# Half as many transfers around a chunked RWKV-7 recurrence: loads by batch, other head pairs, one output transfer

## The chip, the cores and the metric

The kernel runs on one core of a Trainium2 chip. The metric is the device time of one execution in microseconds. The core has TensorE (PE), VectorE (DVE), ScalarE (ACT), GpSimd (POOL) and SyncE (SP), which here only issues transfers; each executes its instructions in order. Sixteen DMA engines move the data.

## The reference

Two parts. An RWKV-7 recurrence over 4 batches, 8 heads, 768 steps, heads of 40, then a feed-forward block with `h * cos(h)`:

```python
for t in range(S):                       # state: (B, H, D, D)
    y[:, :, t] = einsum('bhd,bhde->bhe', r_t, state)
    Sa = einsum('bhde,bhe->bhd', state, a_t)
    state = state * w_t[:, :, None, :] - einsum('bhd,bhe->bhde', Sa, b_t)
    state = state + einsum('bhd,bhe->bhde', v_t, k_t)
x = y.transpose(0, 2, 1, 3).reshape(B * S, H * D)    # 3072 x 320
h = x @ w_in                                         # 320 x 2048
out = (h * cos(h)) @ w_out                           # 2048 x 320
```

The six recurrence inputs are float32; the weights arrive in 64 bits and are converted on the chip.

## The kernel before, in words

The 768 steps are cut into 24 chunks of 32. A chunk holds the 32 steps of all 4 batches on the 128 partitions, and the heads, padded from 40 to 64 columns, in pairs: two heads fill the 128 rows of a transposed tile. In the tiles before, `nat_*` is `[P, 4, 2, 64]`, and the pair `j` consists of heads `j` and `j + 4` for `w`, `a`, `b`, `k` (loaded half by half, line 127), but of neighbours for `v` and `r` (line 122).

- `p1(c)` prepares two chunks without the state: `p1_w` transposes `w` (`wT`) and scans its products (`wp`, `wx`, `wc`); `p1_a` turns them back, takes the reciprocal `rw`, forms `aT` and `bn`; `p1_b` transposes `bn`; `p1_n` multiplies to `nps`, masks it to `nt`, and sends it through a DRAM tile `nd` into `u`, where each partition holds one 32x32 matrix of one head, batch and chunk.
- `inverse(c, part)` inverts the 128 triangular matrices of four chunks at once on VectorE (lines 319 and 323, 31 steps); `inv_end` sends the result through DRAM (`rd`) into `rt`.
- `p2_v`, `p2_k`, `p2_g` bring `k`, `v`, `r` of one chunk: `kn = k * rw` on POOL (line 338), the transposes `vT`, `rT`, `kT`, and the Gram matrices `ag` and the outer parts of `vvm`, in whose middle 40 columns the chunk's `v` stands (a second load of `v`, `load_vv`, line 133).
- `ch_t`, `ch_q`, `ch_x`, `ch_s`, `ch_z` are the chunk proper: they read the state in `qz`, apply `rt` (`sps`, `sm`), write the state back (`dps`; `qz` on VectorE and POOL, lines 480 and 481) and the output `yt` (lines 487 and 492). `yt` goes through a DRAM tile `xd` into `xT`, two chunks to a group (lines 498, 505, 507).
- The feed-forward block is cut into 192 pieces, `first_a`, `first_b` (matmuls `ph`) and two `second` (matmuls `po`) for each of 12 groups and 4 quarters of its columns. The last quarter of a group evicts `po` into `ot` and sends it out (line 556).
- `load_weights` loads 28 blocks of the weights on ACT's queue and converts them on VectorE, ACT and POOL (lines 173 to 191).

The order of TensorE is the program's (`manual_schedule`). Chunk `c` runs its five segments with, between them, `p2_*` of chunk `c + 1`, in the first two of every four chunks `p1` of two chunks of the next four, and then as many feed-forward pieces as are due; a piece of group `g` waits until chunk `2g + 2` is reached. In the third and fourth of every four chunks the next inverse is emitted. The order of the other engines and of SyncE's queue comes from a planner that goes by the instructions' modelled readiness and their place in the program. All transfers but the weights' are issued by SyncE.

Of the kernel before, what the change touches and what calls it, by code (L numbers as in the profile page):

```python
# [9 lines left out]
F32 = mybir.dt.float32  # L10
# [10 lines left out]
def kernel(  # L21
# [77 lines left out]
    def pick(t, offset, *dims):  # L99
# [3 lines left out]
    src = {"r": r, "k": k, "v": v, "w": w, "a": a, "b": b}  # L103

    padding = lambda t: t[:, :, :, D:]
    nat = {
        n: kept(f"nat_{n}", [P, 4, 2, DP], 2, 1.0 if n == "w" else 0.0, padding) for n in "wabkvr"
    }
# [46 lines left out]
    bn_b = kept("bn", [P, 4, 2, DP], 7, 0.0, padding)  # L155
    kn_b = kept("kn", [P, 4, 2, DP], 2, 0.0, padding)
# [75 lines left out]
    unpad = lambda t: t[:, :, :, :D]  # L232
# [44 lines left out]
    def p1_n(c):  # L277
# [20 lines left out]
        nd = dram.tile([P, 2, H, C], F32, tag="nd", name="nd")  # L298
        nc.sync.dma_start(nd.rearrange("p c h t -> p (c h t)"), nt.rearrange("p c e n -> p (c e n)"))
        for i in range(2):  # L300
            for g in range(4):
                p0 = 32 * ((c + i) % 4) + 8 * g
                nc.sync.dma_start(
                    G["u"][p0 : p0 + 8].rearrange("h (s t) -> h s t", s=C),
                    nd[blk[g], i].rearrange("s h t -> h s t"),
                )
# [18 lines left out]
    def inv_end(c):  # L325
        rd = dram.tile([P, C, C], F32, tag="rd", name="rd")
        nc.sync.dma_start(rd.rearrange("p s t -> p (s t)"), G["inv"])
        for i in range(4):
            rt = ring.tile([P, H, C], F32, tag="rt", name="rt")
            for g in range(4):  # L330
                p0 = 32 * i + 8 * g
                nc.sync.dma_start(rt[blk[g]], rd[p0 : p0 + 8].rearrange("h s t -> s h t"))
            G["rt", c + i] = rt


    def p2_v(c):
# [16 lines left out]
    def p2_g(c):  # L353
# [9 lines left out]
        for j in range(4):  # L363
# [13 lines left out]
            pick(vvm[c % 2], C + D, (C, 2), (2 * NV, HH), (1, C)), v1,  # L377
            su.unsqueeze(1).to_broadcast([P, 2, HH, C]), ALU.mult,
        )
        nc.scalar.copy(pick(vvm[c % 2], 0, (2 * NV - C, 2), (2 * NV, HH), (1, C)), v1)  # L380
# [13 lines left out]
    def ch_q(c):  # L394
        ps = at("qps")
        for i in range(2 * B):
            for pa in range(2):
                for e in range(2):
                    mm(
                        ps[full[pa], e, i * C : (i + 1) * C], G["s"][half[e], i, full[pa]],  # L400
                        G["rT", c][half[e], 2 * pa + i % 2, blk[i // 2]], i == 0,
                    )
        nc.scalar.copy(
            pick(qz, 0, (NZ - C, 2), (NZ, 2 * B), (1, C)),
            ps[:, :, : 2 * B * C].rearrange("p e (i t) -> p e i t", t=C),
        )

    def ch_x(c):
        ps = at("x0ps")
        for j in range(4):  # L410
            m, e = j // 2, j % 2
            for bb in range(B):
                for pa in range(2):
                    mm(
                        ps[blk[bb ^ pa], pa, j * N72 : (j + 1) * N72], G["ag", c][blk[bb], 4 * pa + j, :],
                        vvm[c % 2][blk[bb], 4 * pa + j, e * C : e * C + N72], j == 0,
                    )
        if c:
            for j in range(4):
                m, e = j // 2, j % 2  # L420
                for bb in range(B):
                    for pa in range(2):
                        mm(
                            ps[blk[bb ^ pa], pa, j * N72 : (j + 1) * N72],
                            G["aT", c][half[pa], j, blk[bb]],
                            qz[half[pa], bb, m, e * (NZ - N72) : e * (NZ - N72) + N72], False,
# [6 lines left out]
    def ch_s(c):  # L433
        ps = at("sps")
        x0 = G["x0"]
        for j in range(4):
            for bb in range(B):
                for pa in range(2):
                    g = bb ^ pa
                    mm(  # L440
                        ps[blk[bb], pa, j * N72 : (j + 1) * N72], G["rt", c][blk[g], 4 * pa + j, :],
                        x0[blk[g], pa, j * N72 : (j + 1) * N72], j == 0,
# [3 lines left out]
        for pa in range(2):  # L446
            nc.scalar.copy(
                pick(sm[:, pa], 0, (2 * N72, 2), (N72 + C, 2), (1, D)),
                ps[:, pa, : 4 * N72].rearrange("p (m n) -> p m n", m=2)[:, :, C : C + 2 * D].rearrange(
                    "p m (e d) -> p m e d", e=2  # L450
                ),
            )
            nc.vector.tensor_tensor(
                pick(sm[:, pa], D, (2 * N72, 2), (1, 2 * C)),
                pick(ps[:, pa], 0, (2 * N72, 2), (2 * N72 - C, 2), (1, C)),
                su.rearrange("p (m e) t -> p m e t", e=2), ALU.mult,
# [3 lines left out]
    def ch_z(c):  # L460
        ps = [at("dps") for _ in range(2)]
        sm = G["sm"]
        for s, n in ((0, kn_b[c % 2]), (1, bn_b[c % 7])):
            for j in range(4):
                for bb in range(B):
                    for pa in range(2):
                        o = C - C * (j % 2)
                        mm(
                            ps[bb // 2][full[pa], bb % 2, j * N72 : (j + 1) * N72], n[blk[bb], j, pa, :],
                            sm[blk[bb], pa, j, :] if s else vvm[c % 2][blk[bb], 4 * pa + j, o : o + N72],  # L470
# [3 lines left out]
        yt = sb2.tile([P, 4, B, C], F32, tag="yt", name="yt")  # L474
        for i in range(2):
            for bb in range(2 * i, 2 * i + 2):
                dp = ps[i][:, bb % 2]
                if c < NCH - 1:
                    z = pick(qz[:, bb], C, (NZ, 2), (DP, 2), (1, D))
                    nc.vector.tensor_tensor(z, pick(dp, 0, (2 * N72, 2), (N72 + C, 2), (1, D)), z, ALU.add)  # L480
                    nc.gpsimd.tensor_tensor(  # L481
                        z, z,
                        wc.rearrange("p (m e b) -> p m e b", m=2, e=2)[:, :, :, bb]
                        .unsqueeze(3).to_broadcast([P, 2, 2, D]),
                        ALU.mult,
                    )
                nc.vector.tensor_tensor(  # L487
                    yt.rearrange("p (m e) b t -> p m e b t", e=2)[:, :, :, bb],
                    pick(dp, D, (2 * N72, 2), (C, 2), (1, C)),
                    pick(qz[:, bb], 0, (NZ, 2), (NZ - C, 2), (1, C)), ALU.add,  # L490
                )
        nc.gpsimd.tensor_tensor(
# [48 lines left out]
    def second(g, j, i):  # L541
# [44 lines left out]
    with tc.manual_schedule(engines={mybir.EngineType.PE}):  # L586
        for seg in p1(0):
            seg()
        load(0, "kvr")
        load_vv(0)  # L590
        load_vv(1)
        load(2, "wab")
        load(3, "wab")
        for seg in p1(2):
            seg()
        load(4, "wab")
# [8 lines left out]
        START, done, n_seg = 4, 0, 0  # L605
        for c in range(NCH):
# [10 lines left out]
            for i, seg in enumerate(main):  # L617
# [3 lines left out]
                due = (c + (i + 1) / n - START) / (NCH - START) * len(pieces) * 0.97  # L621
# [3 lines left out]
            if c + 2 < NCH:  # L625
                load_vv(c + 2)
# [39 lines left out]
```

## Time and profile before

| | |
|---|---|
| median of 3 runs | 1186.43 us (1184.93 to 1189.02) |
| the profiled execution | 1181.81 us, its span 1180.1 us |
| mean granted TensorE clock | 0.808 |
| busy: PE, DVE, ACT, POOL | 838.5, 507.9, 344.0, 200.8 us (71, 43, 29, 17%) |
| transfers | 270372 packets, 65.68 MB, mean 56 GB/s; 244352 packets under 512 B |
| queue of SyncE and its DMA share | 266112 packets, 52.78 MB, 25.2% of 16 engines |

The span runs from the first to the last instruction; the rest of the execution's time lies around it. Busy shares are means over stages that differ: a start without feed-forward work (to about 180 us), four chunks without it (to about 300 us), the mixed part, and a last group after the last chunk. Matmuls are pipelined, so a busy TensorE is not at its peak.

### The profile page before, as it was taken

To read this page: it belongs to the slowest core of one execution; us is meant where nothing else is said; L and a number is where in the kernel's file an instruction comes from. 1 tells how busy PE (TensorE), PEld (TensorE's weight loads), DVE (VectorE), ACT (ScalarE), POOL (GpSimd) and SP (SyncE) were. 2 spreads that over 40 slices of the span, in tenths; PEclk is the share of its full clock that TensorE was granted. 3 is DMA by queue.
4 is the path that set the end of the run, shared out by engine and by line. 5 is a ranking of instruction groups with operands and counts; after the bars stand their busy time and mean duration, and the time that the engine had idled before them with its cause. 6 is when DMAs were issued, how large, how long until landed. Compare 5 with 4: busy or idle time off the path is not lost.

```text
span 1180.1 us, 37667 instructions
## 1 busy us (share of the span) xinstructions
PE 838.5 (71%) x16472; PEld 644.0 (55%) x16472; DVE 507.9 (43%) x1109; ACT 344.0 (29%) x651; POOL 200.8 (17%) x342
## 2 busy tenths in 40 slices
PE   2140025474688888888987896976977977979878
PEld 1030014363466666665765675755766765757656
DVE  5056985327153375334283335174334292222212
ACT  1011111121233433342432423332422332434323
POOL 1036453121020111111011011011012011020100
PEclk9975555755689988989888998888987986979879
DMA  3434452342412412333213333313332223110000
GB/s 73 61 74 112 118 132 59 49 73 44 85 36 38 80 26 40 82 63 52 51 39 46 76 55 48 58 35 53 74 58 40 52 37 67 35 33 18 16 24 12
DMA packets 270372, 65.68 MB, mean 56 GB/s; under 512 B 244352, under 2 KB 264320, under 8 KB 270208
## 3 DMA queue, kind: packets, MB, share of 16 engines
q1 hardware_dynamic: 266112, 52.78, 25.2%
q10 hardware_dynamic: 4096, 10.49, 2.9%
q8 instruction: 130, 2.13, 0.8%
q14 instruction: 34, 0.28, 0.1%
HBM read 49.02 MB, written 14.16 MB: 54 GB/s over the span
## 4 chain that ended last, share of the span: by engine, by line
PE 41%; SPq 22%; DVE 14%; DMA 7%; issue 7%; ACT 6%; POOL 3%; POOLq 0%; DVEq 0%; ACTq 0%
SPq L127 16%; PE ph L97 15%; PE po L97 13%; DVE inv_tmp L319 2%; DVE inv L323 2%; DVE rw L261 2%; PE x0ps L97 2%; PE dps L97 2%; ACT turns L536 1%; SPq L122 1%; PE bT L226 1%; PE nps L97 1%; PE gram L97 1%; ACT turns L535 1%; DVE wp L245 1%
## 5 line engine op out<-in xcount | busy, mean ns | idle before, releaser
L97 PE MATMUL po<-w_out_sb,gT 128*128 128x320 f32 x768 | 249.3, 479 | 0.0
L97 PE MATMUL ph<-xT,w_in_sb 128*128 128x256 f32 x768 | 202.9, 419 | 18.2 <-DMA xT<-xd 18.1
L97 PEld LDWEIGHTS po<-w_out_sb,gT 128*128 128x128 f32 x768 | 156.2, 211 | 71.6 <-issue 26.4
L97 PEld LDWEIGHTS ph<-xT,w_in_sb 128*128 128x128 f32 x768 | 159.9, 213 | 48.0 <-issue 11.0
L534 DVE SCALAR_TENSOR_TENSOR turns<-turns,ph 128x512 f32<-128x512 f32 x96 | 61.6, 682 | 276.5 <-ACT turns L533 276.5
L533 ACT ACTIVATE turns<-ph,rnd 128x512 f32<-128x512 f32 x96 | 60.7, 684 | 203.1 <-PE ph L97 203.1
L537 DVE TENSOR_TENSOR gT<-ph,turns 128x512 f32<-128x512 f32 x96 | 65.9, 690 | 63.8 <-ACT turns L536 63.5
L481 POOL TENSOR_TENSOR qz<-qz,wc 128x160 f32<-128x160 f32 x92 | 40.5, 461 | 257.4 <-DVE qz L480 257.0
L226 PE MATMUL vT<-ident,nat_v 128*128 128x128 f32 x96 | 18.8, 329 | 78.7 <-DMA nat_v<-in_v_dram 78.7
L319 DVE TENSOR_TENSOR inv_tmp<-u,inv 128x31 f32<-128x31 f32 (+15 forms) x186 | 70.8, 381 | 5.3
L323 DVE TENSOR_TENSOR inv<-inv,inv_tmp 128x31 f32<-128x31 f32 (+15 forms) x186 | 68.1, 366 | 5.0
L536 ACT ACTIVATE turns<-turns,half_pi 128x512 f32<-128x512 f32 x96 | 68.9, 722 | 2.3
L226 PE MATMUL wT<-ident,nat_w 128*128 128x128 f32 x96 | 17.5, 328 | 66.4 <-DMA nat_a<-in_a_dram 57.0
L535 ACT ACTIVATE turns<-turns 128x512 f32<-128x512 f32 x96 | 59.4, 624 | 10.3 <-DVE turns L534 10.3
L249 POOL COPY wx<-wp 128x496 f32<-128x496 f32 x24 | 14.4, 599 | 270.3 <-DVE wp L245 270.3
L338 POOL TENSOR_TENSOR kn<-nat_k,rw 128x320 f32<-128x320 f32 x24 | 21.1, 881 | 225.0 <-PE dps L97 199.0
L245 DVE TENSOR_TENSOR_SCAN wp<-w,w 128x512 f32<-128x512 f32 x24 | 29.8, 1242 | 67.9 <-ACT w L243 66.3
L226 PEld LDWEIGHTS vT<-ident,nat_v 128*128 128x128 f32 x96 | 12.8, 166 | 80.4 <-issue 79.7
L97 PE MATMUL gram<-aT,kT 40*32 40x32 f32 x1536 | 20.5, 226 | 49.1 <-DVE yt L487 33.3
L97 PE MATMUL ph<-xT,w_in_tail 64*128 64x256 f32 x384 | 54.8, 404 | 0.0
L261 DVE RECIPROCAL rw<-wn 128x320 f32<-128x320 f32 x24 | 51.6, 2149 | 4.5 <-PE wn L226 4.2
L226 PEld LDWEIGHTS wT<-ident,nat_w 128*128 128x128 f32 x96 | 12.6, 166 | 69.1 <-issue 63.8
(91 smaller groups left out, 1143.0 us busy)
## 6 DMA issues: line engine op xcount, KB each, us to landing
words<-in_moe_w_out_dram ACTq DMA_DIRECT2D x16, 320.0 KB
words<-in_moe_w_in_dram ACTq DMA_DIRECT2D x8, 512.0 KB
nat_w<-in_w_dram SPq DMA_DIRECT2D x192, 20.0 KB
nat_a<-in_a_dram SPq DMA_DIRECT2D x192, 20.0 KB
nat_b<-in_b_dram SPq DMA_DIRECT2D x192, 20.0 KB
nat_k<-in_k_dram SPq DMA_DIRECT2D x192, 20.0 KB
nat_v<-in_v_dram SPq DMA_DIRECT2D x96, 40.0 KB
nat_r<-in_r_dram SPq DMA_DIRECT2D x96, 40.0 KB
```

Of the source, the lines that this page charges most:

```text
L97: nc.tensor.matmul(o, lhsT=lhsT, rhs=rhs, start=start, stop=stop, skip_group_check=True)
L127: nc.sync.dma_start(t[:, :, e, :D], s[HH * e : HH * (e + 1)].rearrange("j t d -> t j d"))
L226: nc.tensor.transpose(ps[:, i * P : (i + 1) * P], x[:, i].rearrange("p e d -> p (e d)"), ident)
L245: nc.vector.tensor_tensor_scan(flat(wp), flat(w0), flat(w1), 0.0, ALU.mult, ALU.add)
L261: nc.vector.reciprocal(rw, unpad(ps[:, 0].rearrange("p (j a d) -> p j a d", a=2, j=4)))
L319: nc.vector.tensor_tensor(tmp, u[:, :j, j : j + 1].to_broadcast([P, j, C - j]), x[:, j : j + 1, j:].to_broadcast([P, j, C - j]), ALU.mult,)
L323: nc.vector.tensor_tensor(x[:, :j, j:], x[:, :j, j:], tmp, ALU.subtract)
L533: nc.scalar.activation(n, u, ACTF.Identity, bias=rnd, scale=1.0)
L534: nc.vector.scalar_tensor_tensor(n, n, -ROUND, u, ALU.add, ALU.subtract)
L535: nc.scalar.activation(n, n, ACTF.Abs)
L536: nc.scalar.activation(n, n, ACTF.Sin, bias=half_pi, scale=-2.0 * math.pi)
L537: nc.vector.tensor_tensor(G["gT", j][:, 2 * e : 2 * e + 2].rearrange("p f t -> p (f t)"), u, n, ALU.mult)
```

## The change

- Loads: all six inputs of a chunk are loaded with one transfer for each batch (`nat_*` is `[P, 8, ...]`). For `w`, `a`, `b`, `k` the pairs become neighbouring heads, `2j` and `2j + 1`. `v` and `r` are loaded unpadded, and POOL copies them into the padded tiles `vp` and `rp` in another pair order, so that the halves `f` of a pair are heads `i` and `i + 4`. The middle of `vvm` is a POOL copy of `nat_v`; `load_vv` is gone.
- The first loads come in another order: `w` of chunks 0 and 1, `a` of both on ACT's queue, `b`; then `w` of 2 and 3, `a` and `b` of both; `k`, `v`, `r` of chunk 0 only after `p1(2)` is emitted.
- Re-layout: `u`'s partitions are ordered by batch, chunk, head, so one transfer for each batch serves two chunks; `rt` becomes one tile for four chunks with one transfer for each batch.
- Output: one transfer for each output tile. `yt` has one buffer in place of two.
- The due rate of the feed-forward pieces: `SHARE` in place of 0.97.
- The indices of the chunk's matmuls follow the new pairs; their number and shapes stay.

The core of the diff:

```diff
-        n: kept(f"nat_{n}", [P, 4, 2, DP], 2, 1.0 if n == "w" else 0.0, padding) for n in "wabkvr"
+    nat = {n: kept(f"nat_{n}", [P, H, DP], 2, 1.0 if n == "w" else 0.0, padding) for n in "wabk"}
+    nat |= {n: kept(f"nat_{n}", [P, H, D], 2) for n in "vr"}
+    vp, rp = (kept(n, [P, H, DP], 1, 0.0, padding)[0] for n in ("vp", "rp"))
...
-    def load(c, names):
+    def load(c, names, via=nc.sync):
         for n in names:
             for i in range(B):
-                s = src[n][i, :, c * C : (c + 1) * C, :]
-                t = nat[n][c % 2][blk[i]]
-                if n in "vr":
-                    nc.sync.dma_start(
-                        t.rearrange("t i e d -> t (i e) d")[:, :, :D], s.rearrange("h t d -> t h d")
-                    )
-                else:
-                    for e in range(2):
-                        nc.sync.dma_start(
-                            t[:, :, e, :D], s[HH * e : HH * (e + 1)].rearrange("j t d -> t j d")
-                        )
-    def load_vv(c):
...
-    load(0, "wab")
-    load(1, "wab")
+                via.dma_start(
+                    nat[n][c % 2][blk[i], :, :D],
+                    src[n][i, :, c * C : (c + 1) * C, :].rearrange("h t d -> t h d"),
+                )
+    load(0, "w")
+    load(1, "w")
+    load(0, "a", nc.scalar)
+    load(1, "a", nc.scalar)
+    load(0, "b")
+    load(1, "b")
...
-        nd = dram.tile([P, 2, H, C], F32, tag="nd", name="nd")
-        for i in range(2):
-            for g in range(4):
-                p0 = 32 * ((c + i) % 4) + 8 * g
-                nc.sync.dma_start(
-                    G["u"][p0 : p0 + 8].rearrange("h (s t) -> h s t", s=C),
-                    nd[blk[g], i].rearrange("s h t -> h s t"),
-                )
+        nd = dram.tile([P, 2 * H, C], F32, tag="nd", name="nd")
+        for g in range(4):
+            p0 = 32 * g + 8 * (c % 4)
+            nc.sync.dma_start(
+                G["u"][p0 : p0 + 2 * H].rearrange("h (s t) -> h s t", s=C),
+                nd[blk[g]].rearrange("s h t -> h s t"),
+            )
...
-            rt = ring.tile([P, H, C], F32, tag="rt", name="rt")
-            for g in range(4):
-                p0 = 32 * i + 8 * g
-                nc.sync.dma_start(rt[blk[g]], rd[p0 : p0 + 8].rearrange("h s t -> s h t"))
+        rt = sb2.tile([P, 4, H, C], F32, tag="rt", name="rt")
+        for g in range(4):
+            nc.sync.dma_start(
+                rt[blk[g]].rearrange("s c h t -> s (c h) t"), rd[blk[g]].rearrange("h s t -> s h t")
+            )
...
+        for dst, m in ((vp, "v"), (rp, "r")):
+            nc.gpsimd.tensor_copy(
+                dst.rearrange("p (i f) d -> p f i d", f=2)[:, :, :, :D],
+                nat[m][c % 2].rearrange("p (f i) d -> p f i d", f=2),
+            )
+        nc.gpsimd.tensor_copy(vvm[c % 2][:, :, C : C + D], nat["v"][c % 2])
...
-        yt = sb2.tile([P, 4, B, C], F32, tag="yt", name="yt")
+        yt = sb1.tile([P, 4, B, C], F32, tag="yt", name="yt")
...
-                xd[4 * D * e : 4 * D * (e + 1)].rearrange("(j d) t -> d j t", j=4),
+                xd.rearrange("(j e d) t -> e d j t", e=2, d=D)[e],
...
-            for bb in range(B):
-                t0 = bb * S + (2 * g + i) * C
-                nc.sync.dma_start(out[t0 : t0 + C, :], ot[blk[bb], :])
+            t0 = (2 * g + i) * C
+            nc.sync.dma_start(out.rearrange("(b s) n -> b s n", b=B)[:, t0 : t0 + C, :], ot)
...
-        load(0, "kvr")
-        load_vv(0)
-        load_vv(1)
-        load(2, "wab")
-        load(3, "wab")
+        load(2, "w")
+        load(3, "w")
+        load(2, "ab")
+        load(3, "ab")
         for seg in p1(2):
             seg()
+        load(0, "kvr")
...
+        SHARE = len(pieces) * (1 - 1.4 / (NCH // 2)) / (NCH - START)
...
-                due = (c + (i + 1) / n - START) / (NCH - START) * len(pieces) * 0.97
+                due = (c + (i + 1) / n - START) * SHARE
```

## Rows read from the trace of the kernel before

**Rows 1.** The page, part 4: the chain that ended last, shares of the span.
```profile
PE 41%; SPq 22%; DVE 14%; DMA 7%; issue 7%; ACT 6%; POOL 3%; POOLq 0%; DVEq 0%; ACTq 0%
```
**Rows 2.** Waits of TensorE, whole span: waiter <- releaser: us in total, times, longest.
```profile
PE vT L226 <- DMA nat_v<-in_v_dram: 78.7, 4, 61.9
PE wT L226 <- DMA nat_a<-in_a_dram: 57.0, 6, 17.1
PE gram L97 <- DVE yt L487: 33.3, 13, 6.5
PE ph L97 <- DMA xT<-xd: 18.1, 5, 6.9
PE sps L97 <- DMA rt<-rd: 16.5, 3, 15.6
```
**Rows 3.** Windows: stretch, length, busy PE PEld DVE ACT POOL, clock, DMA, GB/s.
```profile
33.40:75.40 42.00, 9.37 (x164) 7.22 (x161) 8.52 (x8) 2.49 (x6) 3.20 (x6) 0.97 0.37 56
...
75.00:180.00 105.00, 13.32 (x444) 10.59 (x438) 81.59 (x173) 18.75 (x35) 59.16 (x84) 0.50 0.47 120
...
266.70:299.90 33.20, 13.13 (x469) 10.50 (x468) 20.22 (x61) 3.99 (x9) 3.98 (x7) 0.50 0.30 46
...
300.00:420.00 120.00, 100.86 (x1906) 77.52 (x1905) 41.61 (x70) 43.37 (x80) 15.47 (x28) 0.88 0.31 57
...
1104.50:1132.50 28.00, 16.21 (x717) 13.38 (x716) 5.07 (x19) 4.09 (x10) 4.27 (x6) 0.60 0.10 28
```
**Rows 4.** Timeline of SyncE's queue: start, us spent on the issues, transfer, count.
```profile
0.81 5.45 SPq L127 DMA_DIRECT2D nat_w<-in_w_dram  x8
...
40.85 4.15 SPq L133 DMA_DIRECT2D vvm<-in_v_dram  x8
...
64.09 3.70 SPq L127 DMA_DIRECT2D nat_b<-in_b_dram  x8
...
78.65 16.84 SPq L303 DMA_DIRECT2D u<-nd  x8
...
164.78 15.48 SPq L332 DMA_DIRECT2D rt<-rd  x16
```
**Rows 5.** Timeline of all engines: start, us, instruction, [idle before, releaser].
```profile
61.85 1.08 PE L226 MATMUL wT<-ident,nat_w 128*128 128x128 f32 x4 [10.25 <-DMA nat_a<-in_a_dram]
...
75.49 0.76 DVE L290 TENSOR_TENSOR nt<-nps,su 128x256 f32<-128x256 f32 x2 [3.17 <-PE nps L97]
...
116.75 0.85 DVE L319 TENSOR_TENSOR inv_tmp<-u,inv 128x31 f32<-128x31 f32 x1
...
166.74 0.41 PE L97 MATMUL sps<-x,rt 32*32 32x72 f32 x2 [15.55 <-DMA rt<-rd]
...
221.72 1.08 PE L226 MATMUL wT<-ident,nat_w 128*128 128x128 f32 x4 [6.18 <-DMA nat_a<-in_a_dram]
...
290.23 1.27 POOL L492 TENSOR_TENSOR yt<-yt,wx 128x512 f32<-128x512 f32 x1
...
299.44 1.09 PE L226 MATMUL vT<-ident,nat_v 128*128 128x128 f32 x4 [6.67 <-DMA nat_v<-in_v_dram]
...
299.87 0.74 SPq L498 DMA_DIRECT2D xd<-yt  x2
...
1132.54 6.22 PE L97 MATMUL ph<-xT,w_in_sb 128*128 128x256 f32 x16 [6.88 <-DMA xT<-xd]
```
**Rows 6.** Waits of TensorE from 300 to 1110 us, those on transfers.
```profile
PE ph L97 <- DMA xT<-xd: 11.3, 4, 5.0
PE vT L226 <- DMA nat_v<-in_v_dram: 10.1, 2, 5.9
...
PE wT L226 <- DMA nat_a<-in_a_dram: 4.7, 1, 4.7
```
**Rows 7.** Groups of POOL by line: out<-in, shapes, count, busy us, mean ns, idle before.
```profile
L338 POOL TENSOR_TENSOR kn<-nat_k,rw 128x320 f32<-128x320 f32 x24 | 21.1, 881 | 225.0 <-PE dps L97 199.0 <-DMA nat_v<-in_v_dram 13.9 <-DMA nat_k<-in_k_dram 9.5
...
L249 POOL COPY wx<-wp 128x496 f32<-128x496 f32 x24 | 14.4, 599 | 270.3 <-DVE wp L245 270.3
```

More of the change, by code (lines that the diff above doesn't have):

```diff
@@ L376, in p2_g @@
         nc.vector.tensor_tensor(
-            pick(vvm[c % 2], C + D, (C, 2), (2 * NV, HH), (1, C)), v1,
+            pick(vvm[c % 2], N72, (HH * NV - N72, 2), (NV, HH), (1, C)), v1,
             su.unsqueeze(1).to_broadcast([P, 2, HH, C]), ALU.mult,
         )
-        nc.scalar.copy(pick(vvm[c % 2], 0, (2 * NV - C, 2), (2 * NV, HH), (1, C)), v1)
+        nc.scalar.copy(pick(vvm[c % 2], 0, (HH * NV + N72, 2), (NV, HH), (1, C)), v1)
         G["ag", c] = ag
@@ L396, in ch_q @@
         for i in range(2 * B):
-            for pa in range(2):
-                for e in range(2):
-                    mm(
-                        ps[full[pa], e, i * C : (i + 1) * C], G["s"][half[e], i, full[pa]],
-                        G["rT", c][half[e], 2 * pa + i % 2, blk[i // 2]], i == 0,
+            for e in range(2):
+                for f in range(2):
+                    mm(
+                        ps[full[e], f, i * C : (i + 1) * C], G["s"][half[f], i, full[e]],
+                        G["rT", c][half[f], 2 * (i % 2) + e, blk[i // 2]], i == 0,
                     )
@@ L410, in ch_x @@
         for j in range(4):
-            m, e = j // 2, j % 2
+            o = C * (j // 2)
             for bb in range(B):
-                for pa in range(2):
+                for e in range(2):
                     mm(
-                        ps[blk[bb ^ pa], pa, j * N72 : (j + 1) * N72], G["ag", c][blk[bb], 4 * pa + j, :],
-                        vvm[c % 2][blk[bb], 4 * pa + j, e * C : e * C + N72], j == 0,
+                        ps[blk[bb ^ e], e, j * N72 : (j + 1) * N72], G["ag", c][blk[bb], 4 * e + j, :],
+                        vvm[c % 2][blk[bb], 2 * j + e, o : o + N72], j == 0,
                     )
@@ L419, in ch_x @@
             for j in range(4):
-                m, e = j // 2, j % 2
+                o = (NZ - N72) * (j // 2)
                 for bb in range(B):
-                    for pa in range(2):
+                    for e in range(2):
                         mm(
-                            ps[blk[bb ^ pa], pa, j * N72 : (j + 1) * N72],
-                            G["aT", c][half[pa], j, blk[bb]],
-                            qz[half[pa], bb, m, e * (NZ - N72) : e * (NZ - N72) + N72], False,
+                            ps[blk[bb ^ e], e, j * N72 : (j + 1) * N72],
+                            G["aT", c][half[e], j, blk[bb]], qz[half[e], bb, j % 2, o : o + N72], False,
                         )
@@ L464, in ch_z @@
             for j in range(4):
+                o = C - C * (j // 2)
                 for bb in range(B):
-                    for pa in range(2):
-                        o = C - C * (j % 2)
-                        mm(
-                            ps[bb // 2][full[pa], bb % 2, j * N72 : (j + 1) * N72], n[blk[bb], j, pa, :],
-                            sm[blk[bb], pa, j, :] if s else vvm[c % 2][blk[bb], 4 * pa + j, o : o + N72],
+                    for e in range(2):
+                        mm(
+                            ps[bb // 2][full[e], bb % 2, j * N72 : (j + 1) * N72],
+                            n[blk[bb], 2 * j + e, :],
+                            sm[blk[bb], e, j, :] if s else vvm[c % 2][blk[bb], 2 * j + e, o : o + N72],
                             s == 0 and j == 0,
@@ L473, in ch_z @@
         wx, wc = G["wx", c], G["wc", c]
-        yt = sb2.tile([P, 4, B, C], F32, tag="yt", name="yt")
[L475 to L490, printed above, removed]
-                )
+        yt = sb1.tile([P, 4, B, C], F32, tag="yt", name="yt")
+        for bb in range(B):
+            dp = ps[bb // 2][:, bb % 2]
+            if c < NCH - 1:
+                z = pick(qz[:, bb], C, (DP, 2), (NZ, 2), (1, D))
+                nc.vector.tensor_tensor(z, pick(dp, 0, (2 * N72 + C, 2), (N72, 2), (1, D)), z, ALU.add)
+                nc.gpsimd.tensor_tensor(
+                    z, z,
+                    wc.rearrange("p (f m b) -> p f m b", f=2, m=2)[:, :, :, bb]
+                    .unsqueeze(3).to_broadcast([P, 2, 2, D]),
+                    ALU.mult,
+                )
+            nc.vector.tensor_tensor(
+                yt.rearrange("p (f m) b t -> p f m b t", f=2)[:, :, :, bb],
+                pick(dp, D, (2 * N72 - D, 2), (N72, 2), (1, C)),
+                pick(qz[:, bb], 0, (NZ - C, 2), (NZ, 2), (1, C)), ALU.add,
+            )
         nc.gpsimd.tensor_tensor(
@@ L603 @@
         load_weights()
-        START, done, n_seg = 4, 0, 0
+        START, done = 4, 0
+        SHARE = len(pieces) * (1 - 1.4 / (NCH // 2)) / (NCH - START)
         for c in range(NCH):
```

59 lines of the change are left out of this document (26 added, 33 removed).

## The prediction

> **What bounds the kernel now.** I read the page's chain first. TensorE carries 41% of it, but SyncE's queue carries 22%, some 260 us, and it does no arithmetic [rows 1]. So part of the span is made by an engine that only issues transfers. Next, TensorE's waits by cause: it stood still 78.7 us for `v`, 57.0 for `a` (the label of a wait in which `w`, loaded just before, is due too), 18.1 for `xT` and 16.5 for `rt`, all transfers; against that stand 33.3 us for VectorE's `yt`, which frees PSUM at the end of a chunk [rows 2]. Then the stretches. From 33.4 to 75.4 us TensorE worked 9.4 of 42 us, from 75 to 180 us 13.3 of 105, while VectorE was busy 81.6 of those 105. From 1104.5 to 1132.5 it worked 16.2 of 28 us [rows 3]. From 300 to 420 us, as in the stretches after it, it worked 100.9 of 120 [rows 3], so there only waits can be won.
>
> Is it the issuing or the moving that is slow? SyncE takes 3.70 us for eight `b` transfers of 20 KB (0.46 each), back to back, and 4.15 us for eight of `vvm`, of 40 KB and twice as many pieces (0.52 each) [rows 4]. The DMA engines are meanwhile busy 0.37 of the time, 0.30 in the later burst [rows 3]. So a transfer costs SyncE about half a microsecond whatever it holds, and the moving has room. The exception is 78 to 180 us, where the weights come in on ACT's queue: eight `u` transfers take 16.84 us, sixteen `rt` 15.48 [rows 4], with the DMA engines still under half busy over that stretch.
>
> **The change, step by step.** By the diff, SyncE issues per chunk 24 loads (six inputs, four batches) instead of 44 (`w`, `a`, `b`, `k` by batch and half, `v` twice); per four chunks 10 re-layout transfers for `u` instead of 18 and 5 for `rt` instead of 17; one per output tile instead of 4. In all some 810 instead of 1482. The matmuls, and VectorE's and ACT's shapes, stay. POOL gets three copies of 128x320 a chunk.
>
> *Step 1, until the second `nt`.* Now the second pair of chunks gets its last `w` at 61.85 and its `nt` at 75.49: a chain of 13.6 us behind the loads [rows 5]. Now the eight `w` transfers of chunks 0 and 1 come first: eight took 5.45 us [rows 4], so they are issued by 6.3 and, with two more to land, there by 8.5. `a` goes on ACT's queue beside them, `b` follows on SyncE by 10.3. The first `nt` is then due at 8.5 + 13.6 = 22. The 24 loads of the second pair need 24 x 0.52 = 12.5 us, `nd` and `u` 2.5: issued by 25.5, landed by 27. `kvr` of chunk 0 no longer stands ahead of them. TensorE is free at 23, so the second `nt` comes between 24 + 13.6 = 38 and 27 + 13.6 = 40.5. Gain 36 us. Bounds: if twice the pieces took twice the issue (0.92 each), the loads end at 54 - 13.6 = 40 and the gain is 21; with nothing in the way it is 39. I take 36, since the `vvm` row is the nearest.
>
> *Step 2, to chunk 0.* The inverse starts at 116.75, 41 us after `nt`, and TensorE then waits 15.55 us for `rt` until 166.74 [rows 5]. `u` comes in 4 transfers of more rows, `rt` in 4 of four times the pieces. Where the weights crowd the queue the pieces count, not the issues, so I don't take the whole 15. VectorE's 81.6 busy us of 105 are the floor, since weights and inverse stay: the gain lies between 0 and 23; I take 12. What is late next is VectorE's weight conversion, behind which `sm` of chunk 0 queues.
>
> *Step 3, chunks 0 to 3* (no MoE pieces run there, nothing covers). TensorE waits 6.18 us for a load at 221.72. At 290.23 POOL multiplies `yt` and is done at 291.5, but `xd` is issued at 299.87, behind a burst of 48 loads and 16 more for k, v, r begun at 266.7; `v` itself is awaited 6.67 us until 299.44 [rows 5]. The burst becomes 36 x 0.52 = 19 us from 266.7, over by 286, so `xd` goes at 291.5 and about 7 us are won. Together 13, bounds 0 (VectorE's inverse, which also works there for 20 of 33 us [rows 3], holds the chunk) and 20.
>
> *Step 4, chunks 4 to 23.* The waits on transfers here are 11.3 us for `xT`, 10.1 for `v` and 4.7 for `a` [rows 6], 26 in all. The `v` and `a` waits should go; `xT` keeps its own two transfer latencies. `load_vv`, which waited on SyncE for `dps` with other loads behind it, becomes a POOL copy. I take 20, bounds 0 and 30.
>
> *Step 5, the end.* MoE pieces now fall due at 192 x 0.97 / 20 = 9.3 a chunk, and the gate (two chunks ready per group) stops them at 176, reached at 18.9 chunks past START: chunk 23 runs almost bare, in 28 us of which 11.8 are idle [rows 3], 6.88 of these waiting for the last `xT` [rows 5]. With SHARE it is 192 x 0.883 / 20 = 8.48 a chunk, 169.6 by the loop's end; 6.4 pieces, some 15 us of work, are left to cover the last `xd` and `xT`, and chunk 23 has its fill. Gain 8, between 4 and 11.8.
>
> *Step 6, what it costs.* No such POOL copy is in the trace. Nearest are the 128x496 copy of `wx`, 599 ns, so 386 scaled to 320 columns, and the 128x320 multiply of `kn`, 881 ns [rows 7]. I take 450: 1.35 us a chunk, 32 in all, on an engine that is busy 15.5 of 120 us from 300 us on [rows 3]. `vp` and `rp` can run as soon as the loads are there. Only the `vvm` copy is released with `kn`, by the `dps` matmuls, and stands ahead of the `qz` multiplies for which the next chunk's transposes wait. I charge 0.3 us x 24 = 7; bounds 0 and 3 x 0.881 x 24 = 63. `yt` with one buffer costs nothing as long as `xd` leaves within a chunk, some 35 us; `rt` of four chunks in two buffers likewise.
> The one output transfer has the four batches as its slowest dimension. The Trainium skill (DMA: Bandwidth & Descriptors, Why a DMA increments its semaphore by 16 and not by 1) says that such a transfer is spread over no more engines than divide that dimension, so over 4; by its 27 GiB/s an engine the last 160 KB would take some 1 us longer, an estimate, and the sum would be 1101. No run here shows it.
>
> Sum against the profiled execution's 1181.8 us (span 1180.1 and 1.7 around it, 0.4% under the median of 1186.4): 36 + 12 + 13 + 20 + 8 - 7 = 82, so **1100 us**.
>
> **Rivals.**
> *More (0.20).* Every step at its upper bound: 39 + 23 + 20 + 30 + 12 = 124, **1058**. For it speaks that SyncE's 260 us of the chain are far more than I claim [rows 1], and that TensorE, at 0.50 of its clock from 75 to 180 us [rows 3], would run faster if fed more densely. Against: in steps 2 and 3 VectorE is close behind.
> *The wait moves (0.20).* With the transfers early, TensorE, which executes in order, meets VectorE's `yt` and the inverse in the same places: steps 3 and 4 give 6 together and step 2 nothing; 36 + 6 + 4 - 7 = 39, **1143**. For it: 33.3 us already go to `yt` [rows 2]. Against: the 57 us at the start have nothing behind them.
> *Pieces, not transfers (0.12).* The pieces stay 160 bytes and their number falls only by `vvm`'s tenth. If the queue backs up at double density (0.37 of the DMA engines would become 0.7), issue times grow towards 0.92: 21 + 0 + 6 + 10 + 8 - 7 = 38, **1144**. For it: 2.1 us per `u` transfer beside the weights [rows 4]. Against: `vvm`'s 0.52. The Trainium skill (DMA: Bandwidth & Descriptors, Bandwidth) calls transfers under 64 KB descriptor-dominated, which is this rival's mechanism; the `vvm` row disagrees as far as issuing goes.
> *Slower (0.05).* POOL executes in order. If the copies stand before `qz` and themselves wait for `v` or `r`, each chunk's end is late by the copies and the wait. From 89 / 24 = 3.7 us a chunk this eats all the rest; copies at 0.881 make 2.6, and a wait of 2 more gives 4.6 x 24 = 110: **1203**. Against: the loads are issued a chunk ahead and SyncE now has room.
>
> **How the numbers follow.** The forecast has 0.43. The range 1055 to 1155 leaves out the slower case, nearly half of the better one and the fringes of the two at 1143. A difference of 0.3% is what a measurement of this kernel can tell. Faster by that: 0.92; within it 0.03 (the two weak cases together with expensive copies); slower 0.05.
>
> **What would show it.** Step 1: `nt` of the second pair before 45 us, and 40 KB transfers at 0.5 us each. Step 2: the 15 us wait for `rt` gone, inverse sooner after `nt`. Steps 3 and 4: TensorE's waits on `v`, `a` under 10 us after 180 us, `xd` right behind `yt`. Step 5: MoE matmuls between the last `dps` and the last `xT`. Step 6: POOL copies of 0.4 to 0.6 us, and `qz` not behind them. Wrong would make me: loads that take 0.8 us each, an inverse that VectorE's order puts no sooner, or TensorE's waits on `yt` growing by what the others lose.

## The result and the profile after

The changed kernel takes 1109.04 us (median of 4 runs, 1102.25 to 1113.92) against 1185.68 for the kernel before on the same chip: a ratio of 0.9352, 95% interval 0.9292 to 0.9411. The forecast was 1100, the range 1055 to 1155. The profiled execution took 1102.25 us, its span is 1100.5. Medians here and below are of all executions; ratios and intervals leave out two that ran in a slower state, one of `e1_share_only` and one of `e5_split_loads`.

The page's chain, which had 22% for SyncE's queue [rows 1], now reads:

```profile
PE 59%; DVE 19%; ACT 8%; DMA 5%; issue 5%; POOL 3%; SPq 1%; ACTq 0%; DVEq 0%; POOLq 0%
```

SyncE's 22% are gone, and VectorE has taken a part of them. TensorE's waits over the whole span say the same with a twist (against [rows 2]):

```profile
PE vT L216 <- POOL vp L331: 46.3, 3, 36.6
PE vT L216 <- POOL rp L331: 43.9, 2, 22.2
PE gram L97 <- DVE yt L481: 41.5, 13, 7.2
PE wn L246 <- DVE sm L447: 20.5, 9, 4.7
...
PE wn L216 <- DMA nat_a<-in_a_dram: 4.1, 2, 3.7
```

The 57.0 us for `a` are 4.1, but the 78.7 for `v` have come back as 90.2 for POOL's copies `vp` and `rp`. Most of this is still a wait for loads, since a copy can't start before its load has landed; some of it is POOL's own order, as the second stage below shows.

The same stages by windows: to the second `nt`, to the first `xd`, to the fourth `xd`, to chunk 23, to the end (columns as in [rows 3]).

```profile
0.00:43.20 43.20, 19.26 (x320) 14.70 (x320) 24.71 (x46) 7.63 (x15) 11.77 (x32) 0.75 0.54 88
43.20:171.20 128.00, 21.30 (x563) 17.50 (x564) 91.62 (x192) 21.29 (x41) 73.29 (x107) 0.50 0.44 108
171.20:260.90 89.70, 57.58 (x1895) 47.33 (x1894) 43.91 (x113) 17.01 (x37) 17.57 (x34) 0.54 0.33 60
260.90:1017.00 756.10, 643.12 (x12999) 493.77 (x12998) 330.51 (x724) 264.57 (x504) 130.00 (x242) 0.88 0.25 49
1017.00:1100.50 83.50, 77.94 (x700) 57.40 (x698) 20.41 (x35) 31.87 (x54) 1.27 (x1) 0.97 0.07 20
```

And the kernel before, cut at the same events:

```profile
0.00:75.50 75.50, 19.32 (x321) 14.82 (x322) 24.85 (x48) 7.60 (x15) 10.50 (x32) 0.98 0.36 62
75.50:197.70 122.20, 22.08 (x563) 18.13 (x564) 91.67 (x192) 21.17 (x41) 68.07 (x98) 0.50 0.43 107
197.70:299.90 102.20, 58.04 (x1902) 47.61 (x1901) 42.95 (x113) 18.45 (x40) 16.10 (x29) 0.57 0.35 59
299.90:1104.50 804.60, 679.65 (x12801) 518.53 (x12800) 332.68 (x723) 275.82 (x517) 101.84 (x177) 0.87 0.27 50
1104.50:1180.10 75.60, 59.37 (x893) 44.91 (x892) 15.73 (x35) 21.01 (x38) 4.27 (x6) 0.81 0.07 20
```

Read the second column down: the first stage is 32.3 us shorter, the second 5.8 us **longer**, the third 12.5 shorter, the last two together (880.2 against 839.6) 40.6 shorter. The last window has 5.6 us without a matmul; the last of before had 16.2. VectorE is busy 91.6 of 128 us in the second stage and 43.9 of 89.7 in the third, so it is not full in either.

What SyncE pays for its issues (against [rows 4]), in its own timeline:

```profile
5.51 6.17 SPq L119 DMA_DIRECT2D nat_b<-in_b_dram  x8
13.14 3.77 SPq L119 DMA_DIRECT2D nat_w<-in_w_dram  x8
...
46.05 4.83 SPq L293 DMA_DIRECT2D u<-nd  x4
54.55 6.96 SPq L119 DMA_DIRECT2D nat_r<-in_r_dram  x4
...
118.16 2.88 SPq L320 DMA_DIRECT2D rt<-rd  x4
123.31 10.77 SPq L119 DMA_DIRECT2D nat_r<-in_r_dram  x3
```

Eight transfers of 40 KB (`w`) take 3.77 us, as eight of 20 KB did before (3.70): 0.47 us each. The eight of `b` at the start, beside `a` on ACT's queue, take 6.17, and beside the weights three transfers of `r` take 10.77.

The second stage by the timeline of all engines (against [rows 5]):

```profile
43.19 0.76 DVE L280 TENSOR_TENSOR nt<-nps,su 128x256 f32<-128x256 f32 x2 [3.17 <-PE nps L97]
...
68.23 0.20 DVE L309 TENSOR_TENSOR inv_tmp<-u,inv 128x31 f32<-128x31 f32 x1
...
122.32 1.11 PE L216 MATMUL vT<-ident,vp 128*128 128x128 f32 x4 [36.57 <-POOL vp L331]
...
145.62 1.11 PE L216 MATMUL vT<-ident,rp 128*128 128x128 f32 x4 [22.19 <-POOL rp L331]
...
149.10 1.25 PE L97 MATMUL sps<-x,rt 32*32 32x72 f32 x64 [1.51 <-ACT rT L342]
...
153.77 0.28 DVE L447 TENSOR_TENSOR sm<-sps,su 128x128 f32<-128x128 f32 x1
...
171.23 0.69 SPq L492 DMA_DIRECT2D xd<-yt  x2
```

`rt` was issued by 121 us. TensorE, in order, stood at the transposes of chunk 1 until 145.62; only then came chunk 0's `sps`. It stood there because `r` of chunk 1 was loaded among the weights and then copied late. The last transfer of `r` was issued at 133.8 and landed at 135.6, by the last update of its semaphore; the copy ran 9.4 us after that, right behind POOL's share of the weights' conversion:

```profile
144.21 0.86 POOL L181 TENSOR_TENSOR w_out_sb<-mant,expo 128x320 f32<-128x320 f32 x1 [0.67 <-DVE expo L178]
145.03 0.54 POOL L331 COPY rp<-nat_r 128x320 f32<-128x320 f32 x1
```

In the same way `rp` of chunk 0 ran at 74.73, 10.9 us after its load had landed at 63.9. So of TensorE's waits of 21.7 and 22.2 us for `rp`, about half is POOL's order and half the load.

What ends this stage is the weights' conversion. The chain that ended last, followed through 43.2 to 171.2 us, has 22% for the weights' transfers, 18% for the inverse, and most of the rest in the conversion on VectorE and POOL:

```profile
by line: DMA words<-in_moe_w_out_dram 13.2%; DVE inv L313 9.2%; DMA words<-in_moe_w_in_dram 8.9%; DVE inv_tmp L309 8.6%; issue 8.0%; DVE mant L168 7.2%; POOL expo L176 7.1%; DVE expo L178 5.9%; POOL expo L177 5.8%; DVE expo L173 4.8%; DVE m
```

The inverse did start 16 us sooner after `nt` than before (25 us instead of 41), and none of it arrived at the end of chunk 0.

The third stage, chunks 1 to 3, ends like this, and in the kernel before `sps` of chunk 3 waited like that:

```profile
251.10 1.24 PE L97 MATMUL sps<-x,rt 32*32 32x72 f32 x62 [7.57 <-DVE x L426]
...
259.64 1.27 POOL L486 TENSOR_TENSOR yt<-yt,wx 128x512 f32<-128x512 f32 x1
...
260.94 0.69 SPq L492 DMA_DIRECT2D xd<-yt  x2
```

```profile
282.30 1.25 PE L97 MATMUL sps<-x,rt 32*32 32x72 f32 x62 [11.07 <-DVE x L430]
```

### The profile page after: what moved, and what is told of

It reads as the page before. It is cut to its first block, busy times and chain, and to the rows that moved or that the text cites. A ratio compares the mean times of both kernels' runs of the same rounds, so it can differ in the third digit from the quotient of the medians.

```text
span 1100.5 us, 36921 instructions
## 1 busy us (share of the span) xinstructions
PE 819.2 (74%) x16472; PEld 630.7 (57%) x16472; DVE 511.2 (46%) x1107; ACT 342.4 (31%) x651; POOL 233.9 (21%) x414
## 4 chain that ended last, share of the span: by engine, by line
PE 59%; DVE 19%; ACT 8%; DMA 5%; issue 5%; POOL 3%; SPq 1%; ACTq 0%; DVEq 0%; POOLq 0%
PE ph L97 20%; PE po L97 19%; DVE inv L313 4%; DVE inv_tmp L309 3%; PE gram L97 3%; DVE rw L251 3%; PE x0ps L97 3%; PE vT L216 2%; ACT turns L529 2%; ACT turns L530 2%; PE sT L385 2%; PE dps L97 2%; PE nps L97 2%; PE bT L216 2%; PE qps L97 2%
## 5 line engine op out<-in xcount | busy, mean ns | idle before, releaser
L97 PE MATMUL ph<-xT,w_in_sb 128*128 128x256 f32 x768 | 198.5, 410 | 0.5 <-issue 0.5
L97 PEld LDWEIGHTS ph<-xT,w_in_sb 128*128 128x128 f32 x768 | 154.7, 207 | 26.6 <-issue 0.9
L313 DVE TENSOR_TENSOR inv<-inv,inv_tmp 128x31 f32<-128x31 f32 (+15 forms) x186 | 73.8, 397 | 5.0
L97 PE MATMUL gram<-aT,kT 40*32 40x32 f32 x1536 | 20.1, 224 | 58.4 <-DVE yt L481 41.5
L239 POOL COPY wx<-wp 128x496 f32<-128x496 f32 x24 | 14.8, 615 | 212.7 <-DVE wp L235 211.4
L97 PEld LDWEIGHTS gram<-aT,kT 40*32 40x32 f32 x1536 | 17.3, 125 | 63.1 <-issue 42.3
L216 PE MATMUL vT<-ident,vp 128*128 128x128 f32 x96 | 18.0, 319 | 46.3 <-POOL vp L331 46.3
L331 POOL COPY vp<-nat_v 128x320 f32<-128x320 f32 x24 | 10.9, 455 | 184.9 <-PE vT L216 72.2
L216 PE MATMUL vT<-ident,rp 128*128 128x128 f32 x96 | 17.2, 310 | 43.9 <-POOL rp L331 43.9
L264 ACT COPY bT<-bT 128x512 f32<-128x512 f32 x24 | 14.0, 585 | 110.8 <-PE bT L216 110.8
```

What stands on the lines that cost most here:

```text
L97: nc.tensor.matmul(o, lhsT=lhsT, rhs=rhs, start=start, stop=stop, skip_group_check=True)
L216: nc.tensor.transpose(ps[:, i * P : (i + 1) * P], x[:, 2 * i : 2 * i + 2].rearrange("p e d -> p (e d)"), ident)
L313: nc.vector.tensor_tensor(x[:, :j, j:], x[:, :j, j:], tmp, ALU.subtract)
```

## The experiments

All are timed against the kernel before on their chip. The changed kernel itself ran once more as a base:

> The changed kernel once more, as the base of the other runs of this chip: 0.929 to 0.941 of the kernel before.

Measured: 1109.92 us, ratio 0.9368 (0.9327 to 0.941). Its profiled execution has a span of 1112.6 us. It sends the fourth `xd` at 260.9 like the first one, and loses its 12 us after that: two executions of one kernel differ by so much in the mixed part, so totals are read by ratio. Up to the fourth `xd` single spans agree better, though not to 0.1 us: `e2_old_due`, edited only from chunk 4 on, sends its fourth `xd` at 258.4, so a difference under some 3 us there is not read as an effect.

**Step 5 alone, and step 5 undone.** `e1_share_only` is the kernel before with the new rate, `e2_old_due` the changed kernel with the old one.

```diff
-                due = (c + (i + 1) / n - START) / (NCH - START) * len(pieces) * 0.97
+                due = (c + (i + 1) / n - START) / (NCH - START) * len(pieces) * (1 - 1.4 / (NCH // 2))
```

> The kernel before with nothing but the new due rate of the feed-forward pieces (0.883 in place of 0.97). If the end is worth what step 5 said, it gains 8 us (1173 to 1179). Theory after seeing the trace: the idle 10.6 us of the tail and the faster clock in chunk 23 together give 15 to 25 us (ratio 0.980 to 0.988). Rival: work moved from the middle to the end leaves as many gaps in the middle as it fills at the end, and nothing is gained (ratio 0.997 to 1.003).

> The changed kernel with the old due rate 0.97. By the theory of e1 it gives the same 15 to 25 us back: 1117 to 1127 in the profiled execution, with TensorE idle some 10 us or more at the end. By the rival nothing changes (1100).

Measured: alone 1177.51 us, 0.9962 (0.9919 to 1.0006), not to be told from nothing; undone 1122.16 us, 0.9487 (0.9441 to 0.9532), 12 to 16 us more than the changed kernel by the medians and by the ratios to its two runs. Undone, the last `xT` is waited for again, 7.0 us. Alone, the tail is filled as well (71.2 us of matmuls in the last 75.5), but TensorE's waits in the middle of `e1_share_only` are these:

```profile
PE vT L226 <- DMA nat_v<-in_v_dram: 19.0, 3, 12.2
...
PE wT L226 <- DMA nat_a<-in_a_dram: 14.2, 2, 8.7
PE wT L226 <- DMA nat_w<-in_w_dram: 8.3, 1, 8.3
```

41.5 us for three inputs where the kernel before has 14.8 for `v` and `a` [rows 6]. With less other work in between, TensorE waits longer for its loads. So what the rate wins at the end goes back to these waits, and it pays clearly only together with fewer transfers; alone, the interval leaves room for up to 10 us.

**Step 2: what holds chunk 0.** Two ways to take chunk 1's loads out of chunk 0's way: `k`, `v`, `r` of chunk 1 emitted early, and all side work of chunk 0 put behind it.

```diff
 # e3_early_kvr1
-        load(c + 1, "kvr") if c + 1 < NCH else None
+        load(c + 1, "kvr") if 1 <= c and c + 1 < NCH else None
...
         load(0, "kvr")
+        load(1, "kvr")
 # e4_chunk0_first
+            if c == 0:
+                late = side
+                side = []
             for i, seg in enumerate(main):
                 seg()
+                if c == 0 and i == 2:
+                    for s in late:
+                        s()
```

> The changed kernel with k, v, r of chunk 1 emitted right behind those of chunk 0, ahead of the loads of chunks 4 and 5. Theory: chunk 0 is late in the changed kernel because TensorE stands 36.6 and 22.2 us at the transposes of chunk 1, whose v and r are loaded behind the weights; with them early the first pieces of sps run when rt is there (about 124 instead of 149 us), chunk 0 ends 10 to 20 us sooner and the whole is 1080 to 1092. Rival: VectorE's conversion of the weights, behind which sm stands, sets chunk 0 anyway: sps is early, sm and the end of chunk 0 are not, and the time stays at 1097 to 1104.

> The changed kernel with all work for chunks 1, 4 and 5 that stood between the segments of chunk 0 put behind chunk 0. Theory (TensorE's order): sps runs at about 124 us without waiting for v and r of chunk 1; chunk 0 ends 15 us sooner, of which chunk 1, which now has that work before it, gives back some 8: 1088 to 1096. Rival (VectorE's conversion sets chunk 0): its end does not move, and the work put behind makes it 1100 to 1110.

Measured: 1103.14 us, 0.931 (0.9248 to 0.9371), and 1098.42 us, 0.9289 (0.9238 to 0.9339). In both `sps` runs when `rt` lands, 20 to 25 us sooner. The timeline of `e4_chunk0_first`:

```profile
121.34 0.42 PE L97 MATMUL sps<-x,rt 32*32 32x72 f32 x2 [35.04 <-DMA rt<-rd]
...
143.07 0.28 DVE L447 TENSOR_TENSOR sm<-sps,su 128x128 f32<-128x128 f32 x1
...
144.88 1.17 PE L97 MATMUL dps<-vvm,kn 32*64 32x72 f32 x52 [18.52 <-DVE sm L447]
```

`sps` is ready at 126 and `sm` runs at 143, behind weight conversions in ACT's and VectorE's order. Chunk 0 sends `xd` at 158.9 in place of 171.2, chunk 3 at 251.5 in place of 260.9. So there were two holds one behind the other: TensorE's wait for chunk 1's `v` and `r`, and the weights' conversions. Of the 20 to 25 us, 3 and 12 reach the end of chunk 0: the rival holds for `e3_early_kvr1`, and `e4_chunk0_first` lies between the two.

**The weights behind chunk 0.** `load_weights()` emitted behind chunk 0 in place of ahead of it; TensorE's order is unchanged. This moves the weights' transfers as well as their conversions.

```diff
-        load_weights()
...
+            if c == 0:
+                load_weights()
```

> The changed kernel with the conversion of the weights emitted behind chunk 0 in place of ahead of it; TensorE's order is the same. Theory (VectorE's conversions, in order ahead of sm, set the end of chunk 0, as the last two runs showed): the inverse starts 15 to 20 us sooner than 68.2, chunk 0 sends xd at 110 to 140 us instead of 171, and the whole gains 15 to 35 us (1065 to 1085), as far as the weights are there when chunk 4 wants them. Rival (the transfers of u, v, r and rt beside the weights set it): chunk 0 not before 160 us, whole 1095 to 1105.

Measured: 1104.11 us, 0.9309 (0.9264 to 0.9355). Chunk 0 does what the theory said, the total doesn't:

```profile
112.09 0.69 SPq L492 DMA_DIRECT2D xd<-yt  x2
...
121.15 0.53 ACTq L163 DMA_DIRECT2D words<-in_moe_w_in_dram  x1
...
154.71 1.12 PE L246 MATMUL wn<-ident,wp 128*128 128x128 f32 x4 [18.71 <-ACT w L233]
```

The first `xd` goes at 112.1, 59 us sooner, so the weights did set chunk 0. This run doesn't say whether by their conversions or by their transfers: all but the first two of these are issued from 121 us on, and with the queue clear the four `u` took SyncE 1.90 us in place of 4.83 and the four `r` 1.96 in place of 6.96. That the conversions hold chunk 0 by themselves shows in `e4_chunk0_first`, where `sm` ran 17 us after `sps` was ready. Now the weights stand in front of chunk 1's side work, and chunk 1 ends at 186.6, chunk 3 at 252.7, only 8 us sooner: their conversion has to be done before chunk 4 in any order.

**Transfers or pieces.** Each load in two by halves of the heads, with the same pieces, 48 loads a chunk.

```diff
-                via.dma_start(
-                    nat[n][c % 2][blk[i], :, :D],
-                    src[n][i, :, c * C : (c + 1) * C, :].rearrange("h t d -> t h d"),
-                )
+                for e in range(2):
+                    hs = slice(HH * e, HH * (e + 1))
+                    via.dma_start(
+                        nat[n][c % 2][blk[i], hs, :D],
+                        src[n][i, hs, c * C : (c + 1) * C, :].rearrange("h t d -> t h d"),
+                    )
```

> The changed kernel with each load of the six inputs in two transfers of 20 KB by halves of the heads: the same pieces, 48 instead of 24 loads a chunk. Theory (SyncE pays by the transfer): the second nt comes some 12 us later than 43.2, the burst before chunk 4 holds xd again, and the whole is 1125 to 1150 us. Rival (the pieces count, not the transfers): 1100 to 1108, issues of 0.25 us each.

Measured: 1123.64 us, 0.9508 (0.9469 to 0.9548), 12 to 17 us over the changed kernel; the intervals don't meet. SyncE's timeline:

```profile
19.84 7.48 SPq L121 DMA_DIRECT2D nat_w<-in_w_dram  x16
...
63.72 14.39 SPq L121 DMA_DIRECT2D nat_r<-in_r_dram  x8
...
133.05 18.19 SPq L121 DMA_DIRECT2D nat_r<-in_r_dram  x7
...
275.35 3.75 SPq L121 DMA_DIRECT2D nat_r<-in_r_dram  x8
279.20 0.71 SPq L494 DMA_DIRECT2D xd<-yt  x2
```

0.47 us a transfer again, now for 20 KB. The second `nt` comes at 51.8 in place of 43.2, and the fourth `xd` goes at 279.2, 18.3 us late: its `yt` was done at 266.9, 6.0 us late, and the other 12.3 it stands behind the loads. This is step 3's picture restored. Beside the weights, `r` of chunk 0 takes 1.80 us a transfer of 20 KB, where it took 1.74 for 40 KB, and `r` of chunk 1 2.60 in place of 3.59: half the pieces don't make half the price there either. The price lies just under the range of the theory, and far from its rival's 0.25 us an issue.

**The first loads' order.** Old order, all on SyncE, 40 KB transfers.

```diff
-    load(0, "w")
-    load(1, "w")
-    load(0, "a", nc.scalar)
-    load(1, "a", nc.scalar)
-    load(0, "b")
-    load(1, "b")
+    load(0, "wab")
+    load(1, "wab")
...
-        load(2, "w")
-        load(3, "w")
-        load(2, "ab")
-        load(3, "ab")
+        load(0, "kvr")
+        load(2, "wab")
+        load(3, "wab")
         for seg in p1(2):
             seg()
-        load(0, "kvr")
```

> The changed kernel with the first loads in the old order, all on SyncE: w, a, b of chunk 0, then of chunk 1; k, v, r of chunk 0 ahead of those of chunks 2 and 3. If the number of transfers makes step 1, the second nt comes at 45 to 50 us in place of 43 to 44, and the time stays within 5 us of the changed kernel's. If the order makes it, nt comes at 55 us or later and the time is 10 to 15 us more.

Measured: 1113.5 us, 0.9374 (0.9343 to 0.9405), the same as the changed kernel within 6 us. `nt` comes at 57.37, 14 us later: so the order, not only the number, makes step 1's landmark. But chunk 0 is 8.5 us later, chunk 3 3.6, and the total the same. Neither branch of the expectation was right as a whole. What is won in front of the weights' stretch does not come out behind it.

**Step 4's second load of `v`, and step 6's copies.** In `e11_vv_by_dma` `load_vv` is back (four transfers a chunk, called as before) and the `vvm` copy is out; in `e6_double_copies` the three copies run twice.

```diff
 # e11_vv_by_dma
-        nc.gpsimd.tensor_copy(vvm[c % 2][:, :, C : C + D], nat["v"][c % 2])
...
+        load_vv(0)
+        load_vv(1)
...
+            if c + 2 < NCH:
+                load_vv(c + 2)
 # e6_double_copies
+        for _ in range(2):
+            for dst, m in ((vp, "v"), (rp, "r")):
...
+            nc.gpsimd.tensor_copy(vvm[c % 2][:, :, C : C + D], nat["v"][c % 2])
```

> The changed kernel with v loaded a second time into vvm, four transfers a chunk on SyncE that wait for dps, in place of the POOL copy. Theory (step 4: this wait held up the loads queued behind it): TensorE's waits on loads come back after chunk 4 and the time is 5 to 15 us more. Rival (with half the transfers the queue has room for such waits): within 4 us of the changed kernel.

> The changed kernel with each of the three POOL copies of a chunk done twice: 1.4 us more of POOL work a chunk. If the copies cost what step 6 said (0.3 us a chunk on the path), this adds 5 to 10 us; if they stand wholly before qz, 1.4 x 24 = 34 us; if POOL's slack covers them, nothing that 3 rounds can tell (under 4 us).

Measured: the second load 1120.79 us, 0.9415 (0.9376 to 0.9454), some 6 us more than the changed kernel by ratio, though the intervals overlap; TensorE's waits on loads did not come back beyond one of 3.9 us, so its mechanism stays open. The doubled copies 1106.43 us, 0.9342 (0.9319 to 0.9364): no cost that can be told. The groups of the copies in the changed kernel (columns as in [rows 7]):

```profile
L335 POOL COPY vvm<-nat_v 128x320 f32<-128x320 f32 x24 | 11.7, 487 | 0.0
L331 POOL COPY rp<-nat_r 128x320 f32<-128x320 f32 x24 | 11.1, 463 | 6.8 <-DMA nat_r<-in_r_dram 3.6 <-DMA nat_w<-in_w_dram 3.2
L331 POOL COPY vp<-nat_v 128x320 f32<-128x320 f32 x24 | 10.9, 455 | 184.9 <-PE vT L216 72.2 <-issue 47.7 <-DMA nat_v<-in_v_dram 33.3
```

**A better version.** TensorE works 57.6 of 89.7 us in the third stage and is the busiest engine of the mixed part, so feed-forward work should begin in the third stage. The same 192 pieces are then spread over 21 chunks, so the rate falls from 8.48 to 8.08 a chunk; the two were not separated.

```diff
-        START, done = 4, 0
+        START, done = 3, 0
```

> The changed kernel with START 3 in place of 4: feed-forward pieces of the first group run from chunk 3 on, 8.1 a chunk. In chunk 3 TensorE has some 10 us of idle time that the pieces can fill; theory: 5 to 12 us less (1097 to 1104). Rival: the pieces stand in TensorE's order ahead of chunk 4's segments and only delay them; no gain.

> START 3 together with the order of e4_chunk0_first (nothing of chunks 1, 4 and 5 between the segments of chunk 0). If the two gains add, 10 to 20 us less than the changed kernel (1089 to 1099); if the start's gain is washed out by the end, the same as the better of the two.

Measured: 1075.38 us, 0.9045 (0.9017 to 0.9073); with the order of `e4_chunk0_first` 1064.31 us, 0.897 (0.8925 to 0.9014), the lowest of all, 4% under the changed kernel. The gain of some 34 us is nearly three times the upper end of what I expected. By the medians the two changes add: 11 us for the order (an interval that meets the base's), 34 for the start, 45 together. Chunk 3, from the third `xd` to the fourth, in the changed kernel and in `e8_start3`, each with one of its groups of matmuls:

```profile
232.80:260.90 28.10, 15.66 (x534) 13.08 (x535) 25.11 (x75) 4.58 (x10) 5.17 (x10) 0.50 0.40 69
...
236.29 1.93 PE L97 MATMUL qps<-rT,s 40*64 40x32 f32 x64 [0.73 <-ACT s L389]
```

```profile
231.90:271.60 39.70, 30.12 (x603) 23.59 (x604) 29.28 (x82) 13.23 (x23) 5.19 (x10) 0.84 0.28 48
...
239.94 1.14 PE L97 MATMUL qps<-rT,s 40*64 40x32 f32 x64
```

The chunk takes 11.6 us longer, and TensorE works 30.1 us of it in place of 15.7. From the third `xd` to the end, with some 14230 matmuls in each, TensorE is busy 736.7 and 735.5 us and idle 131.0 and 144.3 in the two executions of the changed kernel; in `e8_start3` it is busy 719.2 and idle 120.3, in `e10_start3_first` 726.2 and 119.3. So 11 to 25 us are idle time filled, and 9 to 17 us are the same matmuls in less time, as the 64 `qps` above at a granted clock of 0.84 in place of 0.50.

## Why the prediction was right, and where it was not

The total and its main reason hold: SyncE's issue time, half a microsecond a transfer whatever it holds, was on the path, and it is off it now. Step by step, in the profiled execution:

- **Step 1** forecast 36 us, measured 32.3. The queue's cost was as priced (3.77 us for eight). The first `nt` came at 24.8 in place of 22 (the eight `b` took 6.17 us, not 4), the second at 43.2 in place of 38 to 40.5, since TensorE waited 3.71 us for an `a` that stood in SyncE's order behind `nd` and `u`.
- **Step 2** forecast +12, measured -5.8: the step that failed. It took the early `u` and `rt` for a gain and looked only at VectorE behind them. In their place came TensorE's order (chunk 1's transposes ahead of chunk 0's `sps`) and loads of `r` among the weights, shown by `e3_early_kvr1` and `e4_chunk0_first`; and behind that the weights' conversion, which step 2 named as late next, shown by `sm` in `e4_chunk0_first` and, together with the weights' transfers, by `e9_late_weights`.
- **Step 3** forecast 13, measured 12.5. One of its two terms is its mechanism: `xd` goes at 260.94, right behind POOL's `yt`, which ends at 260.91, where it was 8.4 us behind, so this term is 8 and not 7; `e5_split_loads` takes it back. The other term gave nothing. The wait of 6.18 us for a load in chunk 1 is gone, yet from the first `xd` to the second it is 40.3 us in place of 40.8. What made up for it was not forecast: `sps` of chunk 3 waits 7.57 us for VectorE in place of 11.07. That the two came out at 12.5 together is luck.
- **Steps 4 to 6** forecast 20 + 8 - 7 = 21, measured 40.6 in the first profiled execution and 28.5 in the base run (880.2 - 851.7). Step 5 was mis-sized: 12 to 16 us by `e2_old_due`, not 8, and clearly so only on top of the fewer transfers. Step 6 was mis-sized as well: 455 to 487 ns a copy as priced, but by `e6_double_copies` no cost in the total. Its premise that `vp` and `rp` can run as soon as the loads are there failed at the start, where `rp` ran 9 to 11 us after them. Step 4: the waits on loads went as forecast, but a part of the rival came true beside it: the wait of `gram` for `yt` grew from 30.1 to 38.8 us in the mixed part, that of `wn` for `sm` from 11.1 to 18.0.

That the sum came out near is partly luck: step 2 missed by 18 us one way, steps 4 to 6 by 8 to 20 the other. Nor do the stages add up as the forecast added them. `e7_old_order` and `e9_late_weights` move the front by 14 and 59 us and the end by 6 or less. Undone one at a time, the halved loads, the due rate, the `vvm` load and the order give 12 to 17, 12 to 16, about 6 and about 1 us, some 35 of 75. What the re-layout and output transfers give was not tried alone, nor how much comes only from several edits together, as with the due rate; that stays open.

The end bears out the one price that only a page gave. From the last eviction to the end of the span the kernel before took 4.0 us (1176.15 to 1180.1), the changed one 5.1 (1095.41 to 1100.5); their last evictions are:

```profile
1175.73 0.42 ACT L553 COPY ot<-po 128x320 f32<-128x320 f32 x1 [1.73 <-PE po L97]
```

```profile
1094.98 0.43 ACT L547 COPY ot<-po 128x320 f32<-128x320 f32 x1 [1.73 <-PE po L97]
```

The Trainium skill (DMA: Bandwidth & Descriptors, Why a DMA increments its semaphore by 16 and not by 1) has a transfer whose slowest dimension is 4 run on at most 4 engines. The 1.1 us agree with the 1 us estimated by it. They are not chance: in the two kernels traced with four transfers a tile this end takes under 4.0 us, in the twelve traces with one it takes 4.8 to 5.1. In flight at once are at most 15 packets of the last output before and 7 after. It was not tried alone.

The rival of dearer pieces is out where the weights are not moving (0.47 us for 20 KB and for 40). Beside the weights transfers are dear (up to 3.6 us for one of `r`), but not by their pieces alone: with half the pieces each, `e5_split_loads` paid 1.80 for 1.74 and 2.60 for 3.59.

## What to carry to other kernels

Look for an engine in the chain that does no arithmetic, price its instructions by count, and check with the DMA share that the moving has room; then halving the count is a gain that can be forecast. But add up the gains of stages only where the next stage does not wait for something else: here time won in front of the weights' conversion stayed in front of it, and the better lever was to put waiting TensorE work into the thin stretch behind. Before crediting an early arrival, read what the engine that needs it has to execute first, since an in-order engine may stand at another chunk's load.

## What the runs showed of the hardware that was not expected

A granted clock that is read where TensorE hardly works says little about its matmuls. From 43.2 to 171.2 us the changed kernel, `e2_old_due` and `e8_start3` carry out the same instructions; the granted clock reads 0.50 (1.2 GHz) in the first and 1.00 (2.4 GHz) in the other two, yet TensorE is busy 21.3, 21.8 and 21.1 us there, and the four transposes of `rp` at 145 us take 1.11 us in each. Where pieces fill the stretch the same matmuls do get faster: 64 `qps` in 1.14 us in place of 1.93, at 0.84 in place of 0.50. And the same program, in two executions that agree to 0.1 us at the fourth `xd`, ended 12 us apart.
